# A rebuilt account of transfers in the planner of a linear-attention and MLP kernel, and the order chosen anew under it

## The chip, the core and the metric

The kernel runs on one core of one Trainium2 chip. The metric is device time in microseconds (us) of one execution, the median of several. PE is TensorE, DVE is VectorE, ACT is ScalarE, POOL is GpSimd, SP is SyncE, whose queue issues most of the DMA transfers here.

## The reference

Two layers stand behind each other. The first is linear attention with a learned feature map over 8 batches x 8 heads = 64 heads of 576 tokens and 64 channels; the second is layer norm and a two-matrix MLP with a residual, over 8 x 576 = 4608 tokens of width 512.

```python
proj = q_or_k @ w_phi                                   # 64 -> 128
proj = proj - max(abs(proj), axis=-1)
phi  = concatenate([exp(proj), exp(-proj)])             # 256 features
kv   = phi(k)^T v ;  z = sum(phi(k))
attn = (phi(q) kv) / (phi(q) z + 1e-6)
x    = attn, heads side by side                         # (8, 576, 512)
xn   = (x - mean) / sqrt(var + 1e-6) * g_ln
out  = x + relu(xn @ w_ch1) @ w_ch2                     # 512 -> 2048 -> 512
```

## The kernel before

**Attention** is done in 32 units, n = 0 to 31. A unit is two heads of one batch (units 0 to 3 are the heads of batch 0, units 4 to 7 those of batch 1, and so on), with 512 main tokens and 64 tail tokens. For each unit SP's queue loads k, q and v (line 674). k and q are transposed: for units 0 to 7 on PE, from unit 8 on by a DMA transpose on SP's queue (line 919), which reads a bf16 copy `b` that DVE (L893), ACT (L898) or POOL (L900) writes once the loads have landed. PE then makes the products with w_phi: `px` (L941, L942) for the tails, `pm` (L988) for the main tokens, `pt` (L997) the same products the other way round. DVE takes the largest absolute value (`m`, L1045), ACT the exponentials (`ek`, `eb`, `ea`: L1054, L1058, L1065, L1109). POOL scales v by `ek` into `vv` (L1072, L1077, L1078), PE makes kv from it (L1133, L1139) and then `num` (L1197, L1203); DVE divides (`numc`, `rden`: L1219, L1225, L1231) and POOL puts the result into `x` (L1264, L1268), which the text calls a put.

**The MLP** goes by nine groups of four tiles of 128 tokens. Group 0 is the main tokens of batch 0 and needs the puts of the units 0 to 3; group 1 needs those of the units 4 to 7. DVE takes the statistics (`st`, `mv`: L1336, L1348), and `xc`, the centred rows, is written by DVE (L1353), ACT (L1358) or POOL (L1362). It is transposed to `xT`: on PE (L1300) for the groups 0 and 1, by DMA from group 2 on. The first product (L1429, `hT_ps`) has 16 blocks of four matmuls for each group; relu moves a block out of PSUM on ACT (L1439) or DVE (L1437). The second product is L1461 in the groups 0 to 5 and a form with seven products and some sums (L1577, L1586) in the groups 6 to 8. SP's queue stores the result (L1383).

The weights w_ch1 come as two halves of 1 MB (`w`, L767), w_ch2 as two transfers of 1 MB (L785), all on POOL's DMA queue. The second half of w_ch1 is the later one of the two in POOL's order. By the rule `HOLD` the loads of the units 8 to 15 wait on SP until that half has landed.

**The order of the work** is not that of the code. A planner, the class that the listing shows, keeps each operation of the whole kernel with the engines that may do it, its durations there, what it reads and writes, and a rank: the latest start that leaves the rest its time, plus an offset out of the table `OFF` (32 rows by unit, one column by kind of step). It goes through time, gives each engine that comes free the ready operation of the lowest rank, and so fixes both the engine (where several may) and the order on PE, DVE, ACT, POOL and SP. The instructions are then emitted in that order. What the chip does takes as long as it takes: each engine waits for what it needs, in that order. The planner's durations and its account of transfers therefore change nothing on the chip except the order and the choice of engine.

Until the planner's time `WARM` = 75 us PE is given dummy matmuls (L1799, `n_bank<-wz`, 128 columns of zeros by 120) wherever the planner has nothing ready for it: the fillers. They are real instructions with a fixed place in the order.

In the account of transfers each DMA has two parts: the issue on its queue (SP, ACT or POOL) and pieces of about 1.2 us on one of two kinds of queue, `DMA` (SP's and ACT's) and `DMA_w` (POOL's). Each piece takes packets x ns; where both kinds have work their packets take turns. The last piece is followed by a lag until the data count as landed: `LAND`, `LAND_T` for transposes, `LAND_W` for weights, plus terms of a row of `SLACK`. In before, pieces that wait for their kind of queue are served by the time at which they became ready:

```python
                        rank = op.ready if engine in ("DMA", "DMA_w") else op.rank
```

Of the kernel before, what the change touches and what calls it, by code (L numbers as in the profile page):

```python
# [17 lines left out]
def bcast(ap: bass.AP, dim: int, n: int) -> bass.AP:  # L18
# [10 lines left out]
SLACK = ((0.22, 0.0, 0.0, 1.02), (0.35, 0.6, 1.6, 1.03), (0.22, -1.1, 0.0, 1.28))  # L29
# [4 lines left out]
LAND, LAND_T, LAND_W, TURN, BARRIER = 2.8, 1.5, 3.0, 0.004, 0.4  # L34
MIXED, STUCK = 1.5, 0.3
# [3 lines left out]
        "load": 0.0, "trans": 10.1, "trans.copy": 5.5, "mixed": 996.3, "mixed.max": 2.3,  # L39
        "mixed.exp": -5.3, "mixed.fold": 0.0, "k": 13.9, "k.max": 0.0, "k.em": -19.8,  # L40
        "k.exp": -31.1, "en": 0.0, "vv": -168.9, "q": 8.3, "q.max": -6.9, "q.em": 31.7,
        "tails": 138.2, "tails.exp": -252.1, "kv": 37.6, "kv.copy": -11.4, "num0": 49.4,
        "num1": 53.1, "num.dve": -70.6, "g1": 0.0, "g2": 0.0, "g3": 0.0, "put": -0.4, "ln": 0.0,
# [3 lines left out]
        "load": 0.0, "trans": -58.1, "trans.copy": -15.2, "mixed": 93.1, "mixed.max": 63.1,  # L47
        "mixed.exp": 0.0, "mixed.fold": 0.0, "k": 690.9, "k.max": 84.1, "k.em": -37.0,
        "k.exp": 182.4, "en": 0.0, "vv": 10.4, "q": -5.9, "q.max": 42.4, "q.em": -10.7,
        "tails": 0.0, "tails.exp": 119.8, "kv": 0.0, "kv.copy": 2007.2, "num0": 106.9,  # L50
        "num1": 188.8, "num.dve": 26.4, "g1": 0.0, "g2": 0.0, "g3": 0.0, "put": -54.2,
        "ln": 241.8, "w1": 0.0, "w2": 0.0, "ln.c": 0.0, "ln.t": 0.0, "moe": 0.0,
    },
    {
        "load": 0.0, "trans": 32.4, "trans.copy": 3.7, "mixed": -46.2, "mixed.max": -2.9,
        "mixed.exp": -8.2, "mixed.fold": 0.0, "k": 689.0, "k.max": -2.5, "k.em": -155.5,
        "k.exp": -72.9, "en": 0.0, "vv": -1.0, "q": 28.0, "q.max": -11.9, "q.em": 31.7,
        "tails": 1.1, "tails.exp": -34.4, "kv": 60.0, "kv.copy": 1.4, "num0": 1071.9,
        "num1": 70.1, "num.dve": 0.1, "g1": 0.0, "g2": 0.0, "g3": 0.0, "put": 46.8, "ln": 0.0,
# [3 lines left out]
        "load": 0.0, "trans": 0.0, "trans.copy": 73.5, "mixed": 4.7, "mixed.max": -13.2,  # L63
        "mixed.exp": 42.3, "mixed.fold": 0.0, "k": 313.6, "k.max": -4.3, "k.em": -21.4,
        "k.exp": -10.4, "en": 0.0, "vv": 43.3, "q": 43.2, "q.max": -62.4, "q.em": -5.8,
        "tails": 79.9, "tails.exp": 119.5, "kv": 22.2, "kv.copy": -29.7, "num0": 51.1,
        "num1": -59.6, "num.dve": 164.6, "g1": 0.0, "g2": 0.0, "g3": 0.0, "put": 94.3,
        "ln": -399.6, "w1": 0.0, "w2": 0.0, "ln.c": -14.7, "ln.t": 9.3, "moe": 286.1,
    },
    {  # L70
        "load": 251.2, "trans": 368.0, "trans.copy": 94.1, "mixed": -85.8, "mixed.max": -4.5,
        "mixed.exp": 97.8, "mixed.fold": 0.0, "k": 0.0, "k.max": 41.0, "k.em": -10.9,
# [6 lines left out]
        "load": 0.0, "trans": 212.3, "trans.copy": 0.3, "mixed": 73.7, "mixed.max": -316.9,  # L79
        "mixed.exp": 9.8, "mixed.fold": 0.0, "k": 0.0, "k.max": -4.7, "k.em": -21.2,  # L80
        "k.exp": -51.4, "en": 0.0, "vv": -3.6, "q": 0.0, "q.max": -412.1, "q.em": 120.4,
        "tails": 0.0, "tails.exp": 27.1, "kv": -24.4, "kv.copy": 26.9, "num0": 0.0,
        "num1": 15.0, "num.dve": -85.3, "g1": 0.0, "g2": 0.0, "g3": 0.6, "put": 0.0,
        "ln": 245.9, "w1": 0.0, "w2": 0.0, "ln.c": 0.0, "ln.t": 0.0, "moe": 0.0,
    },
    {
        "load": 247.5, "trans": 28.6, "trans.copy": 99.3, "mixed": -0.7, "mixed.max": -0.6,
        "mixed.exp": 0.0, "mixed.fold": 0.0, "k": 0.0, "k.max": 16.4, "k.em": 76.8,
        "k.exp": -1.9, "en": 0.0, "vv": 0.4, "q": 0.0, "q.max": -81.5, "q.em": -0.8,
        "tails": 0.0, "tails.exp": 115.7, "kv": -23.3, "kv.copy": 34.3, "num0": -112.0,  # L90
        "num1": -6.7, "num.dve": 12.3, "g1": 0.0, "g2": 0.0, "g3": 0.0, "put": -30.2, "ln": 0.0,
# [3 lines left out]
        "load": 0.0, "trans": 233.2, "trans.copy": -67.5, "mixed": -95.9, "mixed.max": -2.5,  # L95
        "mixed.exp": 0.0, "mixed.fold": 0.0, "k": 0.0, "k.max": -94.5, "k.em": -50.7,
        "k.exp": 19.6, "en": 0.0, "vv": 8.3, "q": 0.0, "q.max": 10.8, "q.em": 128.4,
        "tails": 0.0, "tails.exp": -225.5, "kv": -19.5, "kv.copy": 23.7, "num0": 116.1,
        "num1": 948.2, "num.dve": 7.5, "g1": 0.0, "g2": 0.0, "g3": -1.0, "put": -30.3,
        "ln": 241.8, "w1": 0.0, "w2": 0.0, "ln.c": -20.4, "ln.t": 22.8, "moe": 288.9,  # L100
    },
    {
        "load": -211.0, "trans": -7.5, "trans.copy": 0.0, "mixed": -0.2, "mixed.max": 7.2,
        "mixed.exp": 137.0, "mixed.fold": 0.0, "k": 0.0, "k.max": 0.0, "k.em": -7.9,
        "k.exp": -7.6, "en": 0.0, "vv": 0.0, "q": 0.0, "q.max": -0.6, "q.em": -150.0,
        "tails": 0.0, "tails.exp": 99.7, "kv": 0.0, "kv.copy": 46.8, "num0": -76.2,
        "num1": -61.8, "num.dve": 14.6, "g1": 346.4, "g2": 0.0, "g3": 0.0, "put": -2.7,
# [3 lines left out]
        "load": 0.0, "trans": -3.4, "trans.copy": 0.0, "mixed": 18.1, "mixed.max": -54.2,  # L111
        "mixed.exp": 43.6, "mixed.fold": 0.0, "k": 0.0, "k.max": 0.0, "k.em": 219.9,
        "k.exp": -17.5, "en": 0.0, "vv": 2.2, "q": 0.0, "q.max": -105.9, "q.em": 0.0,
        "tails": 0.0, "tails.exp": -12.2, "kv": 924.1, "kv.copy": 0.0, "num0": 156.5,
        "num1": -6.7, "num.dve": 73.6, "g1": 0.0, "g2": 0.0, "g3": 180.9, "put": -32.1,
        "ln": 0.0, "w1": 0.0, "w2": 0.0, "ln.c": 0.0, "ln.t": 0.0, "moe": 0.0,
    },
    {
        "load": 9.7, "trans": 2.4, "trans.copy": 0.0, "mixed": -0.7, "mixed.max": 20.2,
        "mixed.exp": -70.2, "mixed.fold": 0.0, "k": 0.0, "k.max": -4.3, "k.em": 0.0,  # L120
        "k.exp": -0.1, "en": 0.0, "vv": 23.6, "q": 0.0, "q.max": 22.2, "q.em": 97.1,
        "tails": 0.0, "tails.exp": 48.6, "kv": 113.4, "kv.copy": -7.0, "num0": -10.1,
# [1716 lines left out]
```

## Time and profile before

| | us |
|---|---|
| median of 3 runs (lowest, highest) | 363.96 (363.77, 365.0) |
| the profiled execution | 363.96 |
| its span, first to last instruction | 362.1 |
| busy in the span: PE, DVE, ACT, POOL | 350.6, 283.9, 256.8, 191.0 |
| fillers in the span | 339 matmuls, 25.8 |

The 1.86 us between the profiled execution's time and its span lie around the program. Times in the views are us from the start of the span. Timeline rows give the start, the duration, the engine, the line and operation, `out<-in`, and a count where equal instructions follow each other; in square brackets the engine's idle time before, and what ended it. Rows of the chain of waits give start, duration, engine, tile and line. In a table by stretches the columns are the stretch, its length, and then for PE, PE's weight loads, DVE, ACT and POOL the busy time with the number of instructions; behind them the granted clock of TensorE, the share of DMA busy, and GB/s. Rows of DMA issues give the median time from issue to landing. DVE works on one thing at a time, POOL too, so that a busy time near the stretch's length means that the engine had nothing to spare.

### The profile page before, as it was taken

The page shows a single profiled execution, that of the slowest core. Times are in us where ns is not written, and L with a number is a line of the kernel's source. Part 1 is how long each engine was busy: PE and PEld are TensorE (multiplying, and loading weights), DVE is VectorE, ACT ScalarE, POOL GpSimd, SP SyncE. Part 2 cuts the span into 40 slices and gives each one's busy share as a digit, 9 for nine tenths or more (in the row PEclk, how much of TensorE's full clock was granted, in tenths as well). Part 3 has the DMA queues.
Part 4 walks back from the last instruction along what each step waited for, and adds up shares of the span by engine and source line. Part 5 has one row for each costly group of instructions (what it writes and reads, how often), then busy time and mean ns, then how long its engine had stood idle before and what let it go on. Part 6 is the DMA issues. An engine that isn't in the chain of part 4 may idle for free.

```text
span 362.1 us, 9154 instructions
## 1 busy us (share of the span) xinstructions
PE 350.6 (97%) x3539; PEld 215.4 (59%) x3564; DVE 283.9 (78%) x605; ACT 256.8 (71%) x555; POOL 191.0 (53%) x243
## 2 busy tenths in 40 slices
PE   8989999998999999999999999999999999999995
PEld 8878764555454655454545555555555567457674
DVE  4799978799997888888889999798777796335363
ACT  3989979498999686969696985796788724751310
POOL 5389546578764694648579798474737310000000
PEclk9999999999999999999999999999999999999999
DMA  8999999999987978389629243931140027200503
GB/s 201 318 219 257 206 257 268 234 312 259 260 214 151 211 163 222 102 154 264 192 70 208 63 106 72 179 91 34 36 120 30 4 42 139 60 2 0 118 0 119
DMA packets 93676, 53.89 MB, mean 149 GB/s; under 512 B 61104, under 2 KB 88048, under 8 KB 93632
## 3 DMA queue, kind: packets, MB, share of 16 engines
q1 hardware_dynamic: 89392, 47.72, 55.9%
q0 software_dynamic: 3328, 4.49, 6.9%
q10 hardware_dynamic: 912, 1.08, 0.9%
q8 instruction: 28, 0.46, 0.5%
q14 instruction: 16, 0.13, 0.1%
HBM read 36.77 MB, written 9.44 MB: 128 GB/s over the span
## 4 chain that ended last, share of the span: by engine, by line
PE 84%; DVE 11%; ACT 3%; issue 1%; POOL 0%; DVEq 0%; ACTq 0%
PE hT_ps L1429 33%; PE ch_ps L1461 20%; PE ch L1577 9%; PE n_bank L1799 4%; PE n_bank L1139 4%; PE pm L988 4%; PE num L1197 3%; DVE m L1045 2%; PE pt L997 2%; DVE st L1336 1%; DVE numc L1219 1%; DVE numc L1225 1%; PE n_bank L1133 1%; ACT eb L1065 1%; DVE o L1586 1%
## 5 line engine op out<-in xcount | busy, mean ns | idle before, releaser
L1429 PE MATMUL hT_ps<-xT,w 128*128 128x512 bf16 x576 | 137.0, 379 | 0.0
L1461 PE MATMUL ch_ps<-w,hT 128*128 128x512 bf16 x363 | 89.8, 379 | 1.3 <-issue 0.3
L1439 ACT ACTIVATE hT<-hT_ps 128x512 bf16<-128x512 f32 x92 | 55.1, 599 | 41.2 <-PE hT_ps L1429 40.1
L1045 DVE TENSOR_REDUCE m<-pm 128x8 f32<-128x1024 f32 x64 | 77.0, 1215 | 7.7 <-PE pm L988 5.6
L1429 PEld LDWEIGHTS <-w 128*128 128x128 bf16 x576 | 51.9, 98 | 52.0 <-issue 1.1
L1072 POOL TENSOR_TENSOR vv<-v,ek 128x1024 bf16<-128x1024 f32 x32 | 61.0, 1906 | 36.9 <-issue 19.9
L1065 ACT ACTIVATE eb<-pm 128x1024 bf16<-128x1024 f32 x64 | 64.2, 1034 | 5.0 <-DVE m L1045 5.0
L1109 ACT ACTIVATE ea<-pt 128x1024 bf16<-128x1024 f32 x64 | 64.4, 1036 | 3.4 <-PE pt L997 1.2
L1264 POOL TENSOR_TENSOR x<-numc,rden 128x128 bf16<-128x128 f32 (+1 forms) x64 | 38.9, 612 | 48.4 <-DVE rden L1231 45.6
L1461 PEld LDWEIGHTS <-hT 128*128 128x128 bf16 x384 | 33.9, 98 | 33.9 <-issue 0.8
L1437 DVE TENSOR_SCALAR hT<-hT_ps 128x512 bf16<-128x512 f32 x52 | 35.7, 687 | 8.5 <-PE hT_ps L1429 8.1
L1197 PEld LDWEIGHTS <-ea 128*128 128x128 bf16 x512 | 24.5, 97 | 10.8 <-issue 1.4
L900 POOL TENSOR_TENSOR b<-qk,one 128x1024 bf16<-128x1024 f32 x13 | 25.0, 1927 | 6.1 <-DMA qkT<-b 3.7
L1139 PE MATMUL n_bank<-vv,eb 128*128 128x65 bf16 x512 | 26.5, 194 | 0.0
L1799 PE MATMUL n_bank<-wz 128*128 128x120 bf16 x339 | 25.8, 228 | 0.1
L1139 PEld LDWEIGHTS <-eb 128*128 128x128 bf16 x512 | 22.2, 98 | 4.6
L1219 DVE TENSOR_TENSOR numc<-num,em 128x390 f32<-128x390 f32 (+1 forms) x40 | 20.2, 512 | 4.8 <-PE num L1197 4.4
L1336 DVE BATCH_NORM_STATS2 st<-x 128x6 f32<-128x512 bf16 (+1 forms) x40 | 21.4, 571 | 1.6 <-POOL x L1264 1.6
L1799 PEld LDWEIGHTS <-wz 128*128 128x128 bf16 x339 | 21.7, 105 | 1.4 <-issue 0.3
L1478 POOL TENSOR_TENSOR o<-o,x 128x512 f32<-128x512 f32 x14 | 16.3, 1162 | 9.9 <-ACT o L1474 8.8
L1225 DVE TENSOR_TENSOR numc<-numc,num 128x390 f32<-128x390 f32 (+1 forms) x40 | 20.5, 518 | 0.6
L1197 PE MATMUL num<-KV,ea 128*128 128x65 bf16 x416 | 19.4, 193 | 1.0 <-DVE KV L1147 0.9
(114 smaller groups left out, 535.7 us busy)
## 6 DMA issues: line engine op xcount, KB each, us to landing
out_dram<-o SPq DMA_DIRECT2D x29, 256.0 KB, 2.5
qk<-in_k_dram SPq DMA_DIRECT2D x12, 512.0 KB, 5.2
qk<-in_q_dram SPq DMA_DIRECT2D x12, 512.0 KB, 6.3
v<-in_v_dram SPq DMA_DIRECT2D x12, 512.0 KB, 4.6
w<-in_moe_w_ch_dram POOLq DMA_DIRECT2D x4, 1024.0 KB, 11.8
qk<-in_k_dram SPq DMA_DIRECT2D x8, 256.0 KB, 6.9
qk<-in_q_dram SPq DMA_DIRECT2D x7, 256.0 KB, 7.4
v<-in_v_dram SPq DMA_DIRECT2D x7, 256.0 KB, 7.7
```

The costliest lines, as they stand in the source:

```text
L1045: nc.vector.reduce_max(out=m, in_=ps, axis=AX.X, apply_absolute_value=True)
L1065: nc.scalar.activation(eb, ps, AF.Exp, scale=(1.0, -1.0)[t])
L1072: eng.tensor_tensor(out=u["vv"][:, :, 0:MX, 0:D], in0=bcast(vb[:, hh, :].rearrange("p (c d) -> p c d", d=D), 1, 2), in1=bcast(e[:, :, 0:MX ...
L1109: nc.scalar.activation(u["EA"][:, t, 0:1024], u["pt"], AF.Exp, scale=(1.0, -1.0)[t])
L1139: nc.tensor.matmul(ps[:, t, c // 4, :], EB[:, t, c, :], vv[:, t, c, :], start=False, stop=(t == 0 and c == MX - 1), skip_group_check=True,)
L1197: nc.tensor.matmul(ps[t][:, i, :], ea(u, t, c), KV[:, t, c // 4, :], start=True, stop=True,)
L1264: eng.tensor_tensor(out=dst, in0=src, in1=by, op=ALU.mult)
L1429: nc.tensor.matmul(st["ps"], w1_sb[:, kc, jj * P : (jj + 1) * P], xT_bufs[g % XB][:, kc::KC, :], start=(kc == 0), stop=(kc == KC - 1),)
L1437: nc.vector.tensor_relu(h_sb, st["ps"])
L1439: nc.scalar.activation(h_sb, st["ps"], AF.Relu)
L1461: nc.tensor.matmul(ch[g, i], hT[g, jj][:, i * P : (i + 1) * P], w2_sb[:, jj, :], start=(jj == 0), stop=(jj == JC - 1),)
L1799: nc.tensor.matmul(warm, wz, wz[:, 0:WN], start=False, stop=False, skip_group_check=True)
```

## The change

The account of transfers is rebuilt, and the offsets of `OFF` are chosen anew under it. In the account: the pieces of a kind of queue are served one transfer behind the other, by the start of their issue; a weight transfer counts in packets of 4 KB (nbytes / 65536 at 0.14 us) in place of the former ones at 0.081; the extra lag for a transfer of SP beside weights (`MIXED`) is gone; the lags and rates are other ones; and from the loads of unit 2 on the first row of `SLACK` holds. Computation, tiles, buffers and DMA sizes stay, and no operation of the work is added or taken away.

```diff
-SLACK = ((0.22, 0.0, 0.0, 1.02), (0.35, 0.6, 1.6, 1.03), (0.22, -1.1, 0.0, 1.28))
+SLACK = ((0.22, 0.0, 0.0, 1.09), (0.35, -1.2, -1.1, 1.03), (0.22, -1.0, 0.0, 1.09))
-LAND, LAND_T, LAND_W, TURN, BARRIER = 2.8, 1.5, 3.0, 0.004, 0.4
-MIXED, STUCK = 1.5, 0.3
+LAND, LAND_T, LAND_W, TURN, BARRIER = 2.7, 1.5, 4.3, 0.021, 0.4
+STUCK = 0.3
 OFF = (
     {
-        "load": 0.0, "trans": 10.1, "trans.copy": 5.5, "mixed": 996.3, "mixed.max": 2.3,
+        "load": 0.0, "trans": 21.9, "trans.copy": -15.2, "mixed": -3.2, "mixed.max": -153.2,
...
 class Move:
-    __slots__ = ("packets", "ns")
-
-    def __init__(self, packets, ns):
-        self.packets, self.ns = packets, ns
+    __slots__ = ("packets", "ns", "by")
+
+    def __init__(self, packets, ns, by):
+        self.packets, self.ns, self.by = packets, ns, by
...
-                        rank = op.ready if engine in ("DMA", "DMA_w") else op.rank
+                        rank = op.us[0].by.start if engine in ("DMA", "DMA_w") else op.rank
...
-                op.engine = engine
+                op.engine, op.start = engine, now
...
-                    if engine == "DMA" and both > 0 and lag > 0:
-                        lag += MIXED
...
-            packets, ns, lag = nbytes / row / 16, 0.081, LAND_W
+            packets, ns, lag = nbytes / 65536, 0.14, LAND_W
...
-        add(queue, us, rank, emit, r=r, w=(key, *w), acquire=lanes, load=(kind, packets * ns))
+        by = add(queue, us, rank, emit, r=r, w=(key, *w), acquire=lanes, load=(kind, packets * ns))
...
-            us=0.65 if queue == "POOL" else 0.53, late=1.7 + 1.4 * (n == 0),
+            us=0.65 if queue == "POOL" else 0.53, late=0.3,
...
-        dma("POOL", -1.5, 8192, gln, w=["gln"], us=0.78, row=4096, late=14.0)
+        dma("POOL", -1.5, 8192, gln, w=["gln"], us=0.78, row=4096, late=1.0)
...
+    sched.slack = SLACK[0]
     for n in range(2, 4):
```

Line numbers of the kernel after are lower by one or two (L1429 is L1427, L1799 is L1798, L1264 is L1262, L900 is L898). On PE 25 fillers fall away; on the other engines some rows go to another engine. Three places of the new order follow; a tile's last number names the buffer.

**First place, POOL, in before,** behind the `vv` of the fourth unit in POOL's order, up to that of the next: `w_132` is the second half of w_ch1, `w_133` are the two transfers of w_ch2, the rows with L1264 and L1268 are puts of the units 2 and 3, the last of which is what the statistics of group 0 wait for.

```order
L767 DMA w_132<-in_moe_w_ch_dram 128x4x1024
L1264 TENSOR_TENSOR x<-numc,rden 128x2x3x64
L1264 TENSOR_TENSOR x<-numc,rden 128x128
L1268 TENSOR_TENSOR xs<-numc,rden 128x64
L785 DMA w_133<-in_moe_w_ch_dram 128x8x512 x2
L1264 TENSOR_TENSOR x<-numc,rden 128x2x3x64
L1264 TENSOR_TENSOR x<-numc,rden 128x128
L1268 TENSOR_TENSOR xs<-numc,rden 128x64
L1264 TENSOR_TENSOR x<-numc,rden 128x2x3x64
L1072 TENSOR_TENSOR vv<-v_105,ek 128x2x8x64
```

The same place on POOL after.

```order
L1262 TENSOR_TENSOR x<-numc,rden 128x2x3x64
L1262 TENSOR_TENSOR x<-numc,rden 128x128
L1266 TENSOR_TENSOR xs<-numc,rden 128x64
L1262 TENSOR_TENSOR x<-numc,rden 128x2x3x64
L765 DMA w_132<-in_moe_w_ch_dram 128x4x1024
L783 DMA w_133<-in_moe_w_ch_dram 128x8x512 x2
L1070 TENSOR_TENSOR vv<-v_105,ek 128x2x8x64
L1075 CAST vv<-ek 128x2x8
L1076 TENSOR_TENSOR vv<-vx_107,ek 128x2x130
L1262 TENSOR_TENSOR x<-numc,rden 128x128
L1266 TENSOR_TENSOR xs<-numc,rden 128x64
L1262 TENSOR_TENSOR x<-numc,rden 128x2x3x64
```

The second half of w_ch1 is issued behind four more puts, and the three instructions of a `vv` now stand ahead of the last three puts.

**Second place, POOL, in before,** where the units 6 and 7 have their `vv` (from `v_101`) and the large bf16 copy of unit 8, `b_2_147<-qk_102`, is made, which unit 8's DMA transpose reads.

```order
L900 TENSOR_TENSOR b_2_147<-qk_102,one 128x1024
L1072 TENSOR_TENSOR vv<-v_101,ek 128x2x8x64
L1077 CAST vv<-ek 128x2x8
L1078 TENSOR_TENSOR vv<-vx_107,ek 128x2x130
L1072 TENSOR_TENSOR vv<-v_101,ek 128x2x8x64
```

The same on POOL after.

```order
L1070 TENSOR_TENSOR vv<-v_101,ek 128x2x8x64
L1075 CAST vv<-ek 128x2x8
L1076 TENSOR_TENSOR vv<-vx_107,ek 128x2x130
L1262 TENSOR_TENSOR x<-numc,rden 128x128
L1266 TENSOR_TENSOR xs<-numc,rden 128x64
L1070 TENSOR_TENSOR vv<-v_101,ek 128x2x8x64
L1075 CAST vv<-ek 128x2x8
L1076 TENSOR_TENSOR vv<-vx_107,ek 128x2x130
L898 TENSOR_TENSOR b_2_147<-qk_102,one 128x1024
```

The copy of unit 8 moved behind both `vv`.

**Third place, PE, in before,** ahead of the sixth block of the first product in group 0: the end of a run of 12 fillers (14 more stand a few rows before), and then unit 6's products (`qkT_143`), of the tails and of the main tokens.

```order
L1799 LDWEIGHTS wz
L1799 MATMUL n_bank<-wz 128x120
L941 LDWEIGHTS qkT_143
L941 MATMUL px<-wbk,qkT_143 128x256
L942 LDWEIGHTS wbk
L942 MATMUL px<-qkT_143,wbk 128x128
L988 LDWEIGHTS qkT_143
L988 MATMUL pm<-wbk,qkT_143 128x128
```

PE after, behind the sixth block: unit 7's tails (`qkT_144`), a filler, unit 6's `pt` and unit 7's `pm`.

```order
L1427 LDWEIGHTS w_132
L1427 MATMUL hT_ps<-xT_138,w_132 128x512
L939 LDWEIGHTS qkT_144
L939 MATMUL px<-wbk,qkT_144 128x256
L940 LDWEIGHTS wbk
L940 MATMUL px<-qkT_144,wbk 128x128
L1798 LDWEIGHTS wz
L1798 MATMUL n_bank<-wz 128x120
L995 LDWEIGHTS wbk
L995 MATMUL pt<-qkT_143,wbk 128x512
L986 LDWEIGHTS qkT_144
L986 MATMUL pm<-wbk,qkT_144 128x128
```

Between the first and the last block of group 0 there are 4 fillers after and 31 before. The pair of unit 6's `pt` and unit 7's `pm` stood behind the twelfth block and stands behind the sixth. Ahead of the first block there are 300 fillers after and 298 before (the 10 at the very start not counted).

More of the change, by code (lines that the diff above doesn't have):

```diff
@@ L46 @@
     {
[L47 to L52, printed above, removed]
-    },
@@ L54 @@
-    {
[L55 to L59, printed above, removed]
+        "load": 0.0, "trans": -32.1, "trans.copy": 0.0, "mixed": -1.4, "mixed.max": -191.2,
@@ L78 @@
     {
[L79 to L84, printed above, removed]
-    },
@@ L86 @@
-    {
[L87 to L91, printed above, removed]
+        "load": 0.0, "trans": 0.0, "trans.copy": 0.0, "mixed": 155.9, "mixed.max": 3.0,
@@ L299 @@
         "engines", "engine", "us", "emit", "rank", "lag", "deps", "users", "acquire", "release",
-        "ready", "left", "number", "due", "load", "cut", "last",
+        "ready", "left", "number", "due", "load", "cut", "last", "start",
     )
 class Move:
-    __slots__ = ("packets", "ns")
-    def __init__(self, packets, ns):
-        self.packets, self.ns = packets, ns
+    __slots__ = ("packets", "ns", "by")
+    def __init__(self, packets, ns, by):
+        self.packets, self.ns, self.by = packets, ns, by
 class Port:
@@ L639, in mm, with dma @@
         return n * (cols / 2.4 + 4.0) / 1000.0
-    def dma(queue, rank, nbytes, emit, r=(), w=(), us=0.53, tiles=0, row=1024, late=1.7):
+    def dma(queue, rank, nbytes, emit, r=(), w=(), us=0.53, tiles=0, row=1024, late=0.3):
         key = ("dma", len(sched.ops))
```

381 lines of the change are left out of this document (199 added, 182 removed), and 33 rows, old and new, of the table OFF.

## Prediction

> **What bounds the kernel now.** I read the page's head and busy times first, then its chain of waits.
>
> ```profile
> span 362.1 us, 9154 instructions
> PE 350.6 (97%) x3539; PEld 215.4 (59%) x3564; DVE 283.9 (78%) x605; ACT 256.8 (71%) x555; POOL 191.0 (53%) x243
> PE 84%; DVE 11%; ACT 3%; issue 1%; POOL 0%; DVEq 0%; ACTq 0%
> L1799 PE MATMUL n_bank<-wz 128*128 128x120 bf16 x339 | 25.8, 228 | 0.1
> ```
>
> PE is busy in 350.6 of 362.1 us and makes 84% of the chain. Two things alone can make the kernel faster: fewer fillers on PE's path (339 of them, 25.8 us, part of it only covers waits), and less idle time of PE, 11.5 us in all. The table by stretches tells where each engine has room.
>
> ```profile
> 30.00:40.00 10.00, 9.99 (x204) 9.04 (x202) 9.85 (x29) 9.60 (x21) 9.36 (x14) 1.00 1.16 241
> 40.00:50.00 10.00, 9.32 (x124) 6.18 (x121) 7.47 (x13) 8.72 (x22) 3.49 (x6) 1.00 1.27 207
> 60.00:70.00 10.00, 9.89 (x108) 5.85 (x108) 6.96 (x12) 5.19 (x12) 5.34 (x5) 1.00 1.22 229
> 70.00:80.00 10.00, 9.95 (x94) 5.24 (x95) 9.69 (x23) 9.89 (x23) 5.84 (x10) 1.00 1.08 270
> 80.00:100.00 20.00, 18.71 (x207) 10.53 (x207) 19.86 (x46) 18.30 (x40) 15.61 (x19) 1.00 1.02 269
> 280.00:310.00 30.00, 29.18 (x250) 19.14 (x248) 22.18 (x57) 15.30 (x28) 5.61 (x9) 1.00 0.36 74
> ```
>
> From 30 to 40 POOL and DVE have no room; from 60 to 70 DVE is starved (6.96 of 10); from 70 to 100 it is full (9.69 of 10, 19.86 of 20), and there PE idles 1.29 us. Between 280 and 310 it idles 0.82 us. What starves DVE from 60 on is unit 8, the first one that is transposed by DMA. The chain of waits in that part:
>
> ```profile
> 50.24 0.73 PE n_bank L1799 x14
> 51.23 0.63 PE n_bank L1799 x12
> 52.58 6.15 PE hT_ps L1429 x28
> 68.66 1.11 DVE m L1045
> ```
>
> The chain goes over two groups of fillers, then over blocks of group 0 (28 matmuls, seven blocks, 6.15 us: 0.88 us each), and at 68.66 to the maximum of unit 8's products.
>
> **The change, part by part.** The sum is made against the profiled execution, 363.96 us, which is also the median of the three runs; 1.86 us of it lie outside the span, and I leave them. About 0.3%, or 1.09 us, is what a measurement of this kernel can tell from no change: faster is below 362.87, slower above 365.05.
>
> *Fillers.* The third place of the order shows the two groups of 14 and 12 gone from PE: 0.73 + 0.63 = 1.36 us, both on the chain. The planner thinks that PE has real work there now (unit 6 and 7's products came forward). If that work isn't ready, PE waits instead and the gain is 0; if it is, 1.36. I take −1.36, since the work is nearly all there at that time on other engines (ACT 8.72 and DVE 7.47 of 10 from 40 to 50, with room). The fillers ahead of the first block are about as many as before (300 against 298), so I count nothing there.
>
> *The weights on POOL, and through them unit 8.* The first place shows the second half of w_ch1 behind four more puts. The rows of POOL and of the transfers at that time:
>
> ```profile
> 29.74 0.79 POOL L767 DMA_DIRECT2D w<-in_moe_w_ch_dram  x1
> 30.55 1.18 POOL L1264 TENSOR_TENSOR x<-numc,rden 128x384 bf16<-128x384 f32 x2
> 31.69 0.29 POOL L1268 TENSOR_TENSOR xs<-numc,rden 128x64 bf16<-128x64 f32 x1
> 35.26 0.82 POOL L1264 TENSOR_TENSOR x<-numc,rden 128x384 bf16<-128x384 f32 x1
> 36.14 1.90 POOL L1072 TENSOR_TENSOR vv<-v,ek 128x1024 bf16<-128x1024 f32 x1
> 37.99 0.26 POOL L1077 CAST vv<-ek 128x16 bf16<-128x16 f32 x1
> 38.14 0.62 POOL L1078 TENSOR_TENSOR vv<-vx,ek 128x260 bf16<-128x260 f32 x1
> 37.91 1.07 DVE L1336 BATCH_NORM_STATS2 st<-x 128x6 f32<-128x256 bf16 x3
> w<-in_moe_w_ch_dram POOLq DMA_DIRECT2D x1, 1024.0 KB, 9.3
> 39.13 1.29 SPq L674 DMA_DIRECT2D qx<-in_k_dram  x2
> q0 software_dynamic: 259, 0.53, 108.5%
> ```
>
> Issued at 29.74, the half lands 9.3 us later, at 39.0, and at 39.13 SP issues the loads of unit 8, which wait for it. The four puts that go ahead now are 1.18 + 0.29 + 0.82 = 2.29 us, so these loads are issued some 2.3 us later. Nothing makes up for that on the transfers' side: the last row is the queue view from 34.2 to 36.8, where POOL's queue alone moves data (259 packets; SP's queue has none), so a later start leaves a hole. What hangs on the loads:
>
> ```profile
> 54.83 1.89 POOL L900 TENSOR_TENSOR b<-qk,one 128x1024 bf16<-128x1024 f32 x1 [1.44 <-DMA qk<-in_q_dram]
> 58.08 3.67 SPq L919 DMA_TRANSPOSE qkT<-b  x1
> qkT<-b SPq DMA_TRANSPOSE x1, 7.4
> qkT<-b SPq DMA_TRANSPOSE x1, 4.5
> 67.84 0.62 PE L988 MATMUL pm<-wbk,qkT 64*128 64x128 bf16 x16
> ```
>
> The bf16 copy starts at 54.83 when q has landed. The transpose is issued at 58.08 and lands 7.4 us later, at 65.5; the next one needs 4.5. PE makes unit 8's products at 67.84, so before nothing waited for the transpose: 2.3 us of slack. Now it lands at 65.5 + 2.3 = 67.8, and PE, without the fillers, is there at 67.84 − 1.36 = 66.5: a wait of 1.3 us. Its bounds are 0 (the transfers make up the delay) and 3.3 (the rival on POOL, below). I take 1.3, since hole and hold are in the rows. DVE, full from 70 to 100, can't win back later what it waits here.
>
> *The puts of unit 3, and the first block.* A `vv` like the one from 36.14 to 38.76 (1.90 and its two small rows) stands now ahead of the last three puts, the last of which ended at 35.26 + 0.82 = 36.08. POOL is busy 9.36 of 10, so up to 2.6 us of delay. The statistics ran at 37.91, 1.8 after the put: 0.8 of it are left. Two `xc` now go on POOL behind each other instead of one, another 1.0 at most. The first block could come 0 to 1.8 us later; then PE comes later to unit 8 too, and the wait of 1.3 there shrinks by as much, so what counts is 0 to 0.5. I take 0.
>
> *Waits further on.* Where PE waited in before:
>
> ```profile
> 83.84 0.79 PE L1300 MATMUL xT_ps<-ident,xc 128*128 128x128 bf16 x11 [0.94 <-DVE xc L1353]
> 85.17 0.40 PE L988 MATMUL pm<-wbk,qkT 64*128 64x128 bf16 x8 [0.21 <-DVE numc L1225]
> 292.54 2.78 PE L1577 MATMUL ch<-w,hT 128*128 128x256 bf16 x24 [0.32 <-DVE numc L1225]
> 295.72 1.03 PE L1577 MATMUL ch<-qk,qk 128*128 128x256 bf16 x8 [0.40 <-DVE o L1586]
> ```
>
> The transposes of group 1 wait 0.94 us for `xc`, products 0.21 for a divide: 1.15. In the new order DVE has about three of its large maxima or copies fewer between unit 8 and these transposes, but it starts no earlier if unit 8 is late. Bounds −1.15 and 0; I take half, −0.6. Near the end 0.32 + 0.40 = 0.72 behind DVE; the order there is nearly the same, with the last divide of the attention moved. Bounds −0.72 and +0.5 (one more such wait); I take −0.35.
>
> Sum: 363.96 − 1.36 + 1.3 − 0.6 − 0.35 = 362.95, so **363.0 us**, A below. Its own range, with the two last terms at both ends and the first two as they are, and up to 0.5 for the puts: 362.0 to 364.9.
>
> **The rivals.**
>
> *B, unit 8 isn't late.* The hole in the transfers is filled, or the loads catch up (SP's queue from 50 on has weights out of its way). Then PE keeps the fillers' gain: 363.96 − 1.36 − 0.6 − 0.35 = 361.65, say 361.7. For it: the copy of q waited 1.44 us on POOL for its load, and transposes were slow (7.4) only behind other loads. Against it: the hold at 39.13 came to the tenth of a microsecond with the landing.
>
> *E, the full stretch opens.* With units 4 to 7 done earlier, DVE and ACT aren't behind from 70 to 100, and PE's idle time there (1.29) and near 300 (0.82) goes as well: 363.96 − 1.36 − 1.29 − 0.82 = 360.5. For it: DVE has 3.04 us to spare from 60 to 70. Against it: that room lies ahead of unit 8, and can be used only if work is there for it.
>
> *C, slower: the copy of unit 8 behind two `vv` on POOL.* The second place shows that it moved behind the `vv` of units 6 and 7.
>
> ```profile
> 61.77 0.21 ACT L1058 ACTIVATE ek<-m 128x12 f32<-128x12 f32 x1
> 62.12 1.91 POOL L1072 TENSOR_TENSOR vv<-v,ek 128x1024 bf16<-128x1024 f32 x1 [2.35 <-issue]
> ```
>
> Unit 7's `vv` came at 62.12, just behind its exponentials at 61.77 to 61.98. POOL takes things in order, so the copy can't start before that `vv` has ended. If the exponentials come forward by no more than the fillers' 1.36, the `vv` starts at 60.8, ends 2.6 later, as the one above, at 63.4, the copy at 65.3, and with the 4.5 of the second transpose the landing is 69.8: PE waits 69.8 − 66.5 = 3.3, and the time is 363.96 − 1.36 + 3.3 = 365.9. Behind it on SP the other transposes queue up, and DVE can't win it back. Against it: the products of unit 7 stand six blocks earlier on PE, 6 x 0.88 = 5.3 us, and with them the exponentials would come at 55.3 and the landing at 64.3, before the 67.8 of the loads. The point from which it decides over A is a start of unit 7's `vv` at 67.8 − 4.5 − 1.9 − 2.6 = 58.8; it gives a slower kernel from a start of about 60.
>
> *D, PE's clock at the start.* By the order, 14 fillers stand ahead of the first transposes instead of 28, and 11 behind them instead of 18. In before:
>
> ```profile
> 1.07 3.01 PE L1799 MATMUL n_bank<-wz 128*128 128x120 bf16 x28
> 4.29 2.01 PE L1799 MATMUL n_bank<-wz 128*128 128x120 bf16 x18
> 7.02 1.11 PE L1799 MATMUL n_bank<-wz 128*128 128x120 bf16 x18
> 8.40 1.63 PE L1799 MATMUL n_bank<-wz 128*128 128x120 bf16 x28
> ```
>
> Until about 7 us a filler takes 108 to 112 ns, from then on about 60. If PE, now with a gap ahead of the first transposes, gets its full rate one such stretch later, the 37 fillers of the later two groups cost up to 37 x 0.05 = 1.9 us more; PE can take most of that out of the idle time between 10 and 30 that the waits for loads leave, so I count a quarter, 0.5: 363.5. [...]
>
> **How the numbers follow.** A 0.33, B 0.25, C 0.22, E 0.14, D 0.06. A leads since hole, hold and slack are all in rows. C has more than its one argument against it leaves, because it needs only one late exponential and POOL's queue has no way round it. Faster are B and E: 0.39. Within 0.3% are A and D: 0.39. Slower is C: 0.22. The range goes from E to C, 360.5 to 365.9; half of each, 0.18, lies beyond.
>
> **What would show it.** In the profile after: no group of 12 fillers between the blocks of group 0 (else the first term is wrong); the second half of w_ch1 issued near 32 and SP's loads held until near 41.4; unit 8's transpose landing near 67.8, with PE idle 1.3 us ahead of its first products. If PE doesn't idle there, it is B or E, told apart by PE's busy time from 80 to 100. If POOL's copy of unit 8 starts after 59, it is C. If the fillers of the first 10 us still take over 100 ns at 8 us, it is D. I am wrong altogether if PE's idle time changes by more than 1 us at some place that none of these names, for instance in the MLP groups from 130 to 280.

## The result and the profile after

| | median us | lowest to highest | runs | ratio to before (95% interval) |
|---|---|---|---|---|
| before | 363.89 | 363.58 to 365.0 | 6 | |
| after | 368.28 | 366.56 to 370.09 | 6 | 1.012 (1.0082 to 1.0158) |

The kernel after is slower by 1.2%. A run more than 1.5% longer than the fastest of its kernel enters no ratio here and below; there were two, one of e1 (368.25 us) and one of before beside e12 (513.46). The profiled execution took 369.89 us with a span of 367.9, so it is one of the longer ones: it shows a loss of 5.8 us of span where the medians differ by 4.4. The head of its page and its chain:

```profile
span 367.9 us, 9109 instructions
PE 351.0 (95%) x3512; PEld 215.0 (58%) x3539; DVE 284.5 (77%) x614; ACT 254.3 (69%) x544; POOL 189.1 (51%) x243
PE 74%; DMA 12%; DVE 7%; ACT 3%; issue 3%; POOL 1%; DVEq 0%; POOLq 0%
```

PE has the same work (351.0 us of it) in a longer span, and 12% of the chain is now DMA, where the chain of before lists none. The stretches of after:

```profile
0.00:10.00 10.00, 7.83 (x84) 7.38 (x85) 4.16 (x20) 3.62 (x5) 4.59 (x12) 1.00 0.81 210
30.00:40.00 10.00, 8.82 (x178) 7.77 (x176) 10.00 (x26) 8.64 (x19) 9.38 (x15) 1.00 1.05 246
60.00:70.00 10.00, 9.76 (x103) 5.33 (x102) 8.00 (x20) 5.74 (x14) 4.53 (x7) 1.00 1.20 207
80.00:100.00 20.00, 19.95 (x206) 11.10 (x205) 18.82 (x42) 17.63 (x37) 13.26 (x18) 1.00 1.16 250
100.00:130.00 30.00, 28.52 (x267) 15.10 (x270) 24.98 (x52) 22.49 (x52) 20.98 (x25) 1.00 0.92 221
130.00:280.00 150.00, 144.48 (x1389) 78.30 (x1403) 120.94 (x239) 113.92 (x247) 89.75 (x109) 0.99 0.55 125
280.00:310.00 30.00, 29.47 (x284) 19.72 (x282) 27.26 (x67) 18.04 (x35) 10.88 (x16) 1.00 0.18 32
```

And the same two middle stretches of before:

```profile
100.00:130.00 30.00, 29.74 (x286) 16.17 (x288) 26.46 (x53) 25.52 (x58) 18.38 (x21) 1.00 0.86 205
130.00:280.00 150.00, 149.15 (x1447) 80.72 (x1460) 125.66 (x247) 117.47 (x263) 102.52 (x124) 1.00 0.53 119
```

From 100 to 280 PE idles 1.48 + 5.52 = 7.00 us in after, against 0.26 + 0.85 = 1.11 in before. Elsewhere the picture is mixed. From 80 to 100 PE idles 0.05 us where it idled 1.29. From 30 to 40, ahead of the late first block, it idles 1.18 us where it idled 0.01, and from 0 to 10 it idles 2.17 where it idled 0.99 and had more fillers. The starts of some blocks of the first product, read off the traces of four kernels (two of them experiments below), tell where each kernel is ahead or behind. (The profiled execution of e1 is its fastest, 362.18 us; that of e12, 384.62, is near its median.)

| block | before | after | four buffers (e1) | before, copies early (e12) |
|---|---|---|---|---|
| group 0, first | 43.48 | 44.85 | 44.52 | 42.81 |
| group 1, first | 86.36 | 84.79 | 84.57 | 87.45 |
| group 1, ninth | 96.36 | 93.77 | 93.54 | 98.10 |
| group 3, first | 161.55 | 163.84 | 158.78 | 174.13 |
| group 4, ninth | 206.73 | 213.93 | 206.19 | 225.59 |
| group 8, first | 318.84 | 324.61 | 317.15 | 339.39 |

After is 1.4 us late at its first block, 2.6 us ahead of before at the ninth of group 1, and 7.2 behind at the ninth of group 4. What happened in between is in the waits of the engines. Each row gives who waited for what: us in total, times, longest. Before, on POOL (ACT and DVE have no such row):

```profile
POOL b L900 <- DMA qkT<-b: 3.7, 3, 2.6
```

After, on POOL, ACT and DVE:

```profile
POOL b L898 <- DMA qkT<-b: 18.6, 8, 4.8
ACT b L896 <- DMA qkT<-b: 9.6, 5, 3.2
DVE b L891 <- DMA qkT<-b: 5.3, 4, 2.5
POOL b L898 <- PE hT_ps L1427: 5.3, 1, 5.3
```

`b` is the bf16 copy of k and q that a DMA transpose reads. It has three buffers, so the copy of unit n may be written only when the transpose of unit n − 3 has read its own. In before the three engines stood 3.7 us at such copies, in after 18.6 + 9.6 + 5.3 = 33.5 us, and whatever is queued behind a copy on its engine stands too. The last row is put down to PE by the profile, but that copy began at 175.43, just behind the landing of a transpose at 175.27, so its 5.3 us probably belong here as well. The chain of after shows two of the places:

```profile
99.81 8.11 DMA qkT<-b
108.08 0.47 POOL b L898
109.93 0.13 POOL vv L1070
...
128.52 7.94 DMA qkT<-b
138.40 1.71 PE hT_ps L1427 x4
```

The first is a transpose in flight for 8.11 us, POOL's copy behind it, and behind that a `vv`; from there the chain goes over POOL and DVE to PE, which waits 1.27 us at 118.12. The second is best seen in the timelines, ACT's first:

```profile
136.48 1.04 ACT L896 CAST b<-qk 128x1024 bf16<-128x1024 f32 x1 [3.16 <-DMA qkT<-b]
137.43 0.37 ACT L1147 CAST KV<-n_bank 128x260 bf16<-128x260 f32 x1
```

and PE's:

```profile
137.85 0.22 PE L1195 MATMUL n_bank<-KV,ea 128*128 128x65 bf16 x2 [2.04 <-ACT KV L1147]
```

ACT stands 3.16 us at a copy until the transpose has landed. The little `KV` cast behind it, 0.37 us, is what PE waits for, 2.04 us. And PE pays again:

```profile
136.00:138.00 2.00, 0.15 (x5) 0.15 (x5) 1.52 (x4) 1.52 (x3) 0.82 (x1) 0.99 0.00 0
138.00:140.00 2.00, 2.00 (x14) 0.88 (x12) 1.43 (x4) 2.00 (x4) 0.42 (x2) 0.50 0.31 78
140.00:142.00 2.00, 2.00 (x20) 1.22 (x19) 1.78 (x3) 0.22 (x2) 0.23 (x1) 0.66 1.07 370
```

Its granted clock is 0.50 and 0.66 in the 4 us behind the pause, about 1.0 + 0.7 = 1.7 us of work lost. 5.9 us of more idle time and 1.7 by the clock are 7.6 us; from the ninth block of group 1 to the end after lost 2.6 + 5.8 = 8.4, so 0.8 us stay open. The fall of the clock is no fixed part of the loss: the mean granted clock was 0.994 and 0.995 in the two longest of the six runs (369.89 and 370.09 us) and 0.998 to 1.0 in the other four (366.56 to 368.76). That may be why the profiled loss is larger than that of the medians.

From 100 to 280 PE itself has no wait for one of these transposes: unit 18's landed at 136.46 and PE made the first products from it at 160.43.

### The profile page after: what moved, and what is told of

Read it like the earlier page. It is cut to its first block, busy times and chain, and to the rows that moved or that the text cites. A ratio compares the mean times of both kernels' runs of the same rounds, so it can differ in the third digit from the quotient of the medians.

```text
span 367.9 us, 9109 instructions
## 1 busy us (share of the span) xinstructions
PE 351.0 (95%) x3512; PEld 215.0 (58%) x3539; DVE 284.5 (77%) x614; ACT 254.3 (69%) x544; POOL 189.1 (51%) x243
## 4 chain that ended last, share of the span: by engine, by line
PE 74%; DMA 12%; DVE 7%; ACT 3%; issue 3%; POOL 1%; DVEq 0%; POOLq 0%
PE hT_ps L1427 29%; PE ch_ps L1459 17%; DMA qkT<-b 10%; PE ch L1575 9%; PE n_bank L1798 4%; PE pm L986 3%; PE n_bank L1137 3%; PE num L1195 3%; PE pt L995 2%; DMA xT<-xc 2%; DVE m L1043 1%; DVE o L1584 1%; DVE numc L1217 1%; ACT ea L1107 1%; PE n_bank L1195 1%
## 5 line engine op out<-in xcount | busy, mean ns | idle before, releaser
L1427 PE MATMUL hT_ps<-xT,w 128*128 128x512 bf16 x576 | 139.0, 382 | 0.2
L1427 PEld LDWEIGHTS <-w 128*128 128x128 bf16 x576 | 51.9, 98 | 52.8 <-issue 2.8
L1063 ACT ACTIVATE eb<-pm 128x1024 bf16<-128x1024 f32 x64 | 65.5, 1036 | 3.2 <-DVE m L1043 2.9
L1262 POOL TENSOR_TENSOR x<-numc,rden 128x128 bf16<-128x128 f32 (+1 forms) x64 | 39.4, 617 | 38.2 <-DVE rden L1229 36.3
L898 POOL TENSOR_TENSOR b<-qk,one 128x1024 bf16<-128x1024 f32 x13 | 24.7, 1903 | 26.0 <-DMA qkT<-b 18.6
L1195 PEld LDWEIGHTS <-ea 128*128 128x128 bf16 x512 | 25.8, 98 | 18.8 <-issue 7.9
L1798 PE MATMUL n_bank<-wz 128*128 128x120 bf16 x314 | 23.7, 228 | 0.0
L1798 PEld LDWEIGHTS <-wz 128*128 128x128 bf16 x314 | 20.1, 105 | 0.8 <-issue 0.3
L1076 POOL TENSOR_TENSOR vv<-vx,ek 128x260 bf16<-128x260 f32 x32 | 19.9, 621 | 0.0
```

What stands on the lines that cost most here:

```text
L1063: nc.scalar.activation(eb, ps, AF.Exp, scale=(1.0, -1.0)[t])
L1195: nc.tensor.matmul(ps[t][:, i, :], ea(u, t, c), KV[:, t, c // 4, :], start=True, stop=True,)
L1262: eng.tensor_tensor(out=dst, in0=src, in1=by, op=ALU.mult)
L1427: nc.tensor.matmul(st["ps"], w1_sb[:, kc, jj * P : (jj + 1) * P], xT_bufs[g % XB][:, kc::KC, :], start=(kc == 0), stop=(kc == KC - 1),)
L1798: nc.tensor.matmul(warm, wz, wz[:, 0:WN], start=False, stop=False, skip_group_check=True)
```

## The experiments

The theory was that the engines' stand at the copies costs the time ("copies"). Its rivals were that the transposes and loads are late in themselves, and that PE's new order asks for things too early. The medians of before were 363.50 to 363.87 us on the four chips of the experiments, so each ratio is to the runs of before on the same chip.

**e1, a fourth buffer.** The order of after, unchanged; the fourth buffer lies in the part of `xm` for the last two pairs of batches, free until then, so from unit 24 on three are used again. A small weight tile moves into a buffer that is free at the start, to make room.

```diff
-    wphi_f = consts.tile([P, F], FP32, name="wphi_f")
+    wphi_f = qx_bufs[1][:, 0].rearrange("p i d -> p (i d)")
...
-    xm = consts.tile([P, NPAIR, DM], BF16, name="xm")
+    xmb = consts.tile([P, NPAIR * DM + P], BF16, name="xm")
+    xm = xmb[:, 0 : NPAIR * DM].rearrange("p (a d) -> p a d", d=DM)
...
+    b16_bufs.append(xmb[:, 2 * DM : 2 * DM + ST])
...
-        b16 = b16_bufs[n % NB16]
+        b16 = b16_bufs[n % 4 if n < 24 else n % 3]
```

> The order of the kernel after, unchanged, with a fourth buffer for the bf16 copies until unit 23 (three from unit 24 on). Theory 'copies': POOL, ACT and DVE, which work in order, stand at a copy until the DMA transpose that reads the same buffer has landed (18.6 + 9.6 + 5.3 us in the kernel after, against 3.7 us in before), and the vv, exponentials and divides queued behind are late for PE. Then these waits go almost wholly, and of the 9.8 us lost between block 8 of group 1 and block 8 of group 4 most come back: 359 to 362 us. Rival 'transfers': the transposes and loads are late in themselves; a further buffer changes nothing: 367 to 369. Rival 'tight order': PE's new order asks for products before DVE and ACT can have done their part, whatever the copies do: 366 to 368.

Measured: 363.08 us (362.18 to 368.25), ratio to before 0.9987 (0.9973 to 1.0002). The waits that are left on ACT and DVE (POOL has none with this name), and one more of POOL:

```profile
ACT b L898 <- DMA qkT<-b: 1.3, 3, 0.7
DVE b L893 <- DMA qkT<-b: 1.5, 2, 1.0
POOL b L900 <- ACT xc L1358: 2.5, 1, 2.5
```

The copies in the fourth buffer stand under the name `xm` and have no such wait. The last row's copy began at 187.00, just behind the landing of a transpose at 186.94, so it may belong here too. 33.5 us of waits fell to 2.8 (with the two doubtful rows, 38.8 to 5.3), and the time by 5.2 us against the median of after: the whole loss. The rivals fall, since neither the transfers' order nor PE's was touched: the work of every engine stands in the same order in both profiles. The expected 359 to 362 was too good.

**e2, the copies later.** Three buffers; in the list in which all engines' instructions are emitted, each copy of the units 11 to 31 moves 18 places back.

```diff
-    place[copy of unit n]
+    place[copy of unit n] + 18        # n = 11 to 31; what depends on it keeps behind it
```

> The order of the kernel after with only the bf16 copies of the units 11 to 31 moved later by 18 places of the list over all engines (some 3 us), and what must stay behind them; PE's order and all buffers as in after. Theory 'copies': the engines do the vv, exponentials and divides first and wait less at the copies: 360 to 364 us. Rival 'transfers': the transposes are issued up to 3 us later and land later, so no better or worse: 368 to 371. Rival 'tight order': 366 to 369.

Measured: 365.31 us (364.11 to 367.08), ratio 1.0056 (1.0035 to 1.0077); what is left of the waits is one row:

```profile
ACT b L859 <- DMA qkT<-b: 0.4, 1, 0.4
```

3 us come back by order alone, with no buffer added. The time misses the 360 to 364 of the theory and is better than both rivals had it. It is not as good as e1, though it has fewer waits; the later copies also put off some loads and transposes that depend on them, which may be why, but no run shows it apart.

**e3 and e4, the two orders one behind the other,** joined at the ninth block of group 1, where after is ahead.

```diff
-    order of after
+    order of after up to the ninth block of group 1, then the order of before for what is left     # e3
+    order of before up to the ninth block of group 1, then the order of after for what is left     # e4
```

> The order of the kernel after up to block 8 of group 1 (where it is 2.6 us ahead of before), then the order of the kernel before for all that is left. Theory 'copies': all of the loss lies behind that point, so the lead stays: 360.5 to 362.5 us. A rival by which the loss comes from the first part (the late weights, the state of buffers and queues that it leaves): 365 to 368.

Measured: 373.71 us (373.45 to 374.03), ratio 1.0273 (1.0251 to 1.0294). It misses both expectations, because of the seam:

```profile
POOL b L861 <- DMA qk<-in_q_dram: 11.3, 1, 11.3
```

POOL stands once for 11.3 us, at a copy whose load of q comes late in the joined order. Up to the first block of group 2 the kernel has lost 8.6 us, and from there to the last group not a tenth more. It tells nothing of the question.

> The order of the kernel before up to block 8 of group 1, then the order of the kernel after for what is left. Theory 'copies': the loss of 8.4 us (from -2.6 to +5.8) comes in the second part alone, so 369 to 373 us, with long waits at the copies. The rival by which the first part is to blame: 362 to 365.

Measured: 367.81 us (367.39 to 370.42), ratio 1.0125 (1.0084 to 1.0166). The copies wait again, 24.7 us in all, and the kernel is 4.1 us slower than before, less than the 5 to 9 that were expected:

```profile
POOL b L861 <- DMA qkT<-b: 14.4, 5, 5.8
ACT b L859 <- DMA qkT<-b: 6.9, 3, 3.3
DVE b L854 <- DMA qkT<-b: 3.4, 3, 1.5
```

So the second part of the new order loses time without the first part, with its late weights, ahead of it. It loses 4.4 us of span here and 8.4 in after; how much of the difference is the state that it starts from stays open.

**e5, e6 and e7, the account and the table apart.**

```diff
 OFF = ...                                                  # e5: account of after, table of before
 OFF = ...                                                  # e6: account of before, table of after
-SLACK = ((0.22, 0.0, 0.0, 1.09), (0.35, -1.2, -1.1, 1.03), (0.22, -1.0, 0.0, 1.09))
+SLACK = ((0.22, 0.0, 0.0, 1.09), (0.35, -1.2, 1.6, 1.03), (0.22, -1.0, 0.0, 1.09))   # e7, else as after
```

> The new account of transfers with the table of offsets of the kernel before. Theory 'copies, by the account': the new account counts a transpose as landed 2.7 us earlier than the old one (its extra lag goes from +1.6 to -1.1), so the planner puts each bf16 copy that much too close behind the transpose that must have read its buffer, whatever the table: POOL, ACT and DVE wait at the copies for 25 us or more in all, and the time is 367 to 373 us. Rival 'by the table': the offsets chosen anew pull the copies forward, and with the old table the copies wait as little as in before (under 8 us): 362 to 366.

> The old account with the new table of offsets. Theory 'copies, by the account': waits at the copies under 10 us in all, 362.5 to 366 us (no table was chosen for this pair, which may cost something elsewhere). Rival 'by the table': waits of 25 us and more, 367 to 370.

> The kernel after with one number of its account put back: the extra lag of a DMA transpose from unit 6 on is +1.6 as in before instead of -1.1; the planner makes its order anew under the new table. Theory 'copies, by the account': waits at the copies fall below 10 us, and the time to 361.5 to 365.5 us. Rival: it is the queueing one behind the other or the packets of the new account that set the copies, and this number alone does little: 367 to 369.

Measured: 417.2 us (ratio 1.1466, 1.143 to 1.1501), 407.37 us (1.121, 1.1167 to 1.1252) and 417.64 us (1.1477, 1.1437 to 1.1517). All three expectations of the time are missed, by 37 to 49 us: neither table is worth anything under an account that it was not chosen for, and one changed number was enough for that (e7). What such an order loses, it loses all over the kernel (e7 is 7 us behind before at the first block, 34 at group 5, 50 at group 7). Where in detail stays open. The waits at the copies can still be compared. In e5, with the new account:

```profile
POOL b L898 <- DMA qkT<-b: 4.4, 3, 2.9
ACT b L896 <- DMA qkT<-b: 4.5, 5, 2.3
DVE b L891 <- DMA qkT<-b: 5.7, 4, 2.8
```

In e7, with one number of it put back:

```profile
POOL b L898 <- DMA qkT<-b: 0.9, 2, 0.6
ACT b L896 <- DMA qkT<-b: 0.2, 1, 0.2
DVE b L891 <- DMA qkT<-b: 1.2, 1, 1.2
```

14.6 us with the new lag, 2.3 with the old one, and 4.4 in e6, under the old account. That points to the account's lag for a landed transpose as what pulls the copies forward, but e5 misses both expectations of its waits (25 and more, or under 8), and in kernels that are some 45 us longer the copies have more time in any case. The orders themselves say it more plainly, since no time on the chip enters them. Count the places in the list of all instructions as they are emitted: from unit 19 on, the median copy stands 36 places behind the transpose that frees its buffer in before, 24 in after, 20 in e5, 33 in e6 and 32 in e7. With the new lag the copies stand near under either table, with the old one far under either, and e7 differs from after by this number alone. So it is the lag that pulls the copies forward, and hardly the table, which moves them by some four places.

**e8, a control:** the four buffers of e1 under the order of before.

```diff
-        b16 = b16_bufs[n % NB16]
+        b16 = b16_bufs[n % 4 if n < 24 else n % 3]
```

> The order of the kernel before with the fourth buffer for the copies, as a control. Its copies wait 3.7 us, on POOL alone. Theory 'copies': little to win, 363.0 to 363.9 us. Rival: the changed layout of memory or more room for copies makes any order faster by several us, so that the four buffers tell nothing of the new order: 358 to 361.

Measured: 364.07 us, ratio 1.0002 (0.9985 to 1.0019), a little above the expected range, as before itself had 363.87 beside it. All through the profile the first and ninth blocks start within 0.02 us of those of before. The buffer helps only an order that stands at the copies.

**e9, e10 and e11, the way to unit 8,** which the prediction had made its main term, on top of e1.

```diff
 # e9, POOL
+L765 DMA w_132 (second half of w_ch1), ahead of unit 2's puts
+L783 DMA w_133 x2 (w_ch2), behind unit 2's first puts
 # e10, DVE and PE
+L1308 xT x4, ahead of unit 5's maximum L1043 and the exponential that needs it
-L1798 fillers, 26 between group 0's transposes and its first block
 # e11: both
```

> The kernel of the fourth buffer (new order), with the first place on POOL partly undone: the second half of w_ch1 and the two transfers of w_ch2 stand where they stood in before, ahead of the puts; the vv of unit 4 stays where the new order has it. By the steps of the prediction: unit 8's transpose lands some 2 us earlier (65.5 to 66.5 instead of 67.9), the 0.3 us that PE waits there go, no more, because PE comes to it only near 67.9 (its first block is 1 us later than in before): 0 to 0.5 us faster than the kernel of the fourth buffer, so 362.5 to 363.2. Rival: the late weights cost more than that wait shows, since DVE is full from 70 to 100: 1 to 2 us faster, 361 to 362.

Measured: 363.36 us (362.25 to 363.62), ratio 0.9982 (0.997 to 0.9993). Unit 8's transpose landed at 66.38, 1.5 us earlier than in e1, and PE's wait for it was gone; the first block of group 1 started at 85.00 (e1: 84.57). The time lies just above what both expectations gave. No gain is seen, but the first block of group 0 came later too (45.41 against 44.52), so a small one may be hidden. It is the one version that beats before beyond its interval, by 0.2%, which is less than the 0.3% by which the prediction tells a change from none.

> The kernel of the fourth buffer with the first block of group 0 let go earlier: a maximum of unit 5 on DVE (1.2 us) moves behind the four copies of group 0's transposes, with the exponential that needs it, and the 26 fillers between those transposes and the first block are left out. The weights stay late. The first block comes 0.7 to 1 us earlier. By the steps of the prediction PE then waits that much longer for unit 8's transpose (landing 67.9): 0 to 0.3 us faster, 362.8 to 363.3. Rival: the first block sets the time, unit 8's transpose doesn't: 0.7 to 1 us faster, 362.0 to 362.4, and no longer wait at unit 8.

> Both edits: weights first, and the first block of group 0 let go earlier. By the steps of the prediction the two stand one behind the other on the way to unit 8, so that only both together gain: 0.8 to 1.3 us faster than the kernel of the fourth buffer, 361.8 to 362.4, and about 1.5 us faster than before. Rival: DVE, full from 70 to 100, takes the gain back: 362.8 to 363.3.

Measured: 364.59 us (ratio 1.002, 1.0005 to 1.0036) and 363.73 us (1.0009, 0.999 to 1.0027). The edit failed to do what it was for: the first block started at 44.69 in e10 and at 46.24 in e11, not ahead of e1's 44.52. Besides, in e10 PE waits once for 2.50 us behind DVE, a wait that e1 does not have.

```profile
111.19 0.53 PE L1159 MATMUL num<-KV,ea 128*128 128x65 bf16 x12 [2.50 <-DVE m L1007]
```

These two leave open what an earlier first block would be worth.

**e12, the copies early in before.** The order of before; each copy of the units 11 to 31 moves 18 places forward, as far as its load and the transpose that frees its buffer allow. Nothing else of the change is in it.

```diff
-    place[copy of unit n]
+    place[copy of unit n] - 18        # n = 11 to 31; order of the kernel before
```

> The order of the kernel before with only the bf16 copies of the units 11 to 31 moved forward by 18 places of the list over all engines (some 3 us), as near behind the transposes as the new order has them; three buffers; PE's and SP's order unchanged. Theory 'copies': POOL, ACT and DVE now wait at the copies, 10 to 30 us in all where before had 3.7, and the time is 366 to 371 us, a good part of the change's loss without the change. Rival 'something else of the new order': the copies alone do little, 363.5 to 365 us.

Measured: 384.65 us (383.8 to 386.72), ratio 1.0591 (1.0546 to 1.0637):

```profile
POOL b L861 <- DMA qkT<-b: 13.1, 4, 6.1
ACT b L859 <- DMA qkT<-b: 8.0, 4, 3.2
DVE b L854 <- DMA qkT<-b: 8.4, 2, 5.0
```

29.5 us of waits and 21.2 us more time, beyond what the theory expected: the copies alone, moved in the kernel before, lose more than the change does. What the copies overtook on their engines came later too, and how much of the 21.2 us is that, no run shows apart. But e1 takes the waits out of the order of after and the loss goes, e8 shows that the buffer by itself is worth nothing, and e12 puts the waits into the order of before and a loss comes. Together they show that the waits at the copies cost the time.

## Why the prediction was wrong

Forecast was 363.0, range 360.5 to 365.9; the kernel came out at 368.28. By its steps:

**Fillers, −1.36.** Right: the two groups are gone, and the work put in their place was ready, since PE was busy for the whole of 40 to 60. The next point took some of it back: after started its first block 1.37 us late and was 0.79 ahead at the ninth block of group 0 (54.32 against 55.11).

**The puts of unit 3, 0 to 1.8, taken as 0.** The mechanism was right, and the delay of the first block came inside its bounds, near the upper one. In after:

```profile
32.55 0.79 POOL L765 DMA_DIRECT2D w<-in_moe_w_ch_dram  x1
35.12 1.94 POOL L1070 TENSOR_TENSOR vv<-v,ek 128x1024 bf16<-128x1024 f32 x1
38.30 0.82 POOL L1262 TENSOR_TENSOR x<-numc,rden 128x384 bf16<-128x384 f32 x1
39.74 2.04 POOL L1360 TENSOR_TENSOR xc<-mv,x 128x512 bf16<-128x512 f32 x2 [0.62 <-DVE mv L1346]
```

The last put ended at 39.12 instead of 36.08, the two `xc` at 41.78, and the first block came 1.37 us later. Taking 0 for the sum did no harm, because the wait in the next point shrank by about as much.

**Unit 8, a landing at 67.8 and a wait of 1.3.** The landing was 68.12 and the wait 0.18: PE was as late as the transpose, by the point above, as the prediction said it would be if the puts were late. PE's row in after, and the copy of unit 8 on POOL:

```profile
68.17 0.28 PE L939 MATMUL n_bank<-wbk,qkT 128*128 128x256 bf16 x1 [0.18 <-DMA qkT<-b]
```

```profile
58.23 1.89 POOL L898 TENSOR_TENSOR b<-qk,one 128x1024 bf16<-128x1024 f32 x1
```

The copy began at 58.23, ahead of 59, so by the prediction's sign it was not C. That the landing came so near to 67.8 is partly luck. The second half of w_ch1 landed at 40.65 instead of 39.08, 1.6 us later and not 2.3; the load of q for unit 8 then took 12.5 us where it had taken 12.3, was issued at 45.00 instead of 42.49, and landed 2.8 later; and the copy stood another 0.7 us behind a `vv` on POOL, which is the step of C.

**Waits further on, −0.6 and −0.35.** The two places named did as forecast or better: from 80 to 100 the idle time fell by 1.24 us, from 280 to 310 from 0.82 to 0.53 (the stretches go by the time from the start; after was up to 2.6 us ahead in the first and some 5.8 behind in the second). What the term left out is the error, below.

**D, the clock at the start.** Not so by the prediction's sign: in the chain of after, fillers take 100 ns each at 6.4 and 57 ns at 8.2. The granted clock reads 1.00 from 0 to 10 in both kernels, so the slower fillers of the first 7 to 8 us don't show in it, and what makes them slow stays open. That a gap ahead of the first transposes puts the faster fillers off was the author's assumption. After has such a gap, 1.17 us up to 3.85, and its fillers were still slow from 6.39 to 7.79, where those of before took 62 ns from 7.02; that the gap made them so, no run shows apart.

```profile
6.39 1.40 PE n_bank L1798 x14
8.21 1.02 PE n_bank L1798 x18
```

Without the waits at the copies the sum of all these is e1: 363.08 us against the forecast 363.0. That they agree to a tenth is in part luck too, since the single terms came out as much as a microsecond off, in both directions.

**The step that failed** is the term "Waits further on": it listed the waits that PE had in before, near 84 and near 293, and put all that might come between 100 and 280 at nothing, without a reason. There PE idled 7.00 us in after against 1.11. The list of places has the same gap. "The second place" looked at one copy, that of unit 8, and only asked whether it was too late. That copies behind it could be too early for their buffers, and that POOL, ACT and DVE would stand in order behind them (33.5 us instead of 3.7), was in no term, no bound and no rival; the prediction's own last sentence, that it would be wrong altogether if PE's idle time changed from 130 to 280, is what came true (144.48 busy instead of 149.15). Two things in hand would have shown it. The page of before has POOL's copies idle "<-DMA qkT<-b 3.7": the wait was there, small, with nothing said of how near it was to being large. And in the order, from unit 19 on, a copy stands 30 to 51 places of the emission list behind the transpose that frees its buffer in before, and 19 to 37 in after. A lag in the account that falls by 2.7 us (from +1.6 to −1.1) for every such transpose was in the diff, and it was read as a matter of the planner only.

## What to carry to other kernels

When a change makes a planner think that transfers land sooner, look first at every instruction that may start only after a landing, and at what is queued behind it on its engine; the one that waits needn't be the one that is needed. A buffer that is reused every third time is such a wait, though nothing of the data is late. Where an order is written out by rule, an added buffer under the same order is the cleanest test: it takes one wait away and moves nothing.

## What the runs showed of the hardware

PE's granted clock fell behind a pause of PE in two kernels and stayed up behind a slightly longer one in a third. In after PE stood 2.04 us ahead of the products at 137.85, and the clock was granted at 0.50 from 138 to 140 and at 0.66 from 140 to 142; four matmuls of a block took 1.71 us there, where four take 0.86 at the first block of group 1 in the same chain:

```profile
84.95 0.86 PE hT_ps L1427 x4
```

The pause and the slow work behind it cost some 3.7 us. In e12 a pause of 2.48 us ended at 189.53, and the clock was granted at 0.50 from 190 to 192 (its mean from 150 to 200 was 0.93). But in e10 the clock stayed at 1.00 behind the pause of 2.50 us that ended at 111.19:

```profile
111.20:115.00 3.80, 3.80 (x37) 1.96 (x37) 3.66 (x11) 1.91 (x8) 3.40 (x6) 1.00 0.77 263
```

So these runs give no length of a pause from which the clock falls; the one of 2.04 us in after cost nearly twice its length.

A transpose's time from issue to landing ran from 3.2 to 8.1 us in after. What was queued ahead of it on SP's queue differed: the one issued at 99.81 took 8.11 behind two loads and four stores, the one issued at 99.70 in before 3.66 behind a transpose and one store. No run varies the queue alone, so that it is the queue that makes the difference is not shown.
